# Two feed-forward layers behind banded attention on one core: another split of the tokens into chunks, and a shorter lag at the last chunk

## Chip, core and metric

The kernel runs on one NeuronCore of a Trainium2 chip. The metric is the device time of one execution in microseconds (us). PE is the matmul engine, PEld its weight loads, DVE the vector engine, ACT the scalar engine, POOL is GpSimd, and SP issues the DMAs.

## What is computed

Attention over a band of 128 keys with a linear bias (4 batches, 8 heads, 576 tokens, head size 64), then two feed-forward layers over all 2304 tokens (model width 512; hidden widths 1536 and 2048):

```python
scores = scale * np.matmul(q, k.transpose(0, 1, 3, 2))
mask = (rel >= 0) & (rel < window)                  # window = 128
scores = np.where(mask, scores + bias[None], -1000000000.0)
attn = softmax(scores)                              # over the keys
x = np.matmul(attn, v)                              # as (2304, 512)
g = x @ w_gate                                      # first layer
x = (g * sigmoid(g) * (x @ w_val)) @ w_out
h = x @ w_in                                        # second layer
y = (h * np.tanh(softplus(h))) @ w_out2
```

## The kernel before

**Layout.** The 2304 tokens lie in one row, 576 to a batch. `A_CHUNKS` (L26) cuts this row into five chunks, which attention and the first layer work off one after the other. Within a chunk, `chunk_plan` cuts queries into blocks of at most 128 that never cross a batch border; a query block sees its own 128 keys and the block ahead of it. The second layer works on three parts of 768 tokens (`TB = 384`) and is not touched.

**Attention of a chunk** (`attention`), for each of eight heads: scores (`score`; PE tile `s_ps`), a predicated copy on DVE that folds the two key blocks into one (L219 for a pair of blocks, L226 for one), a reduction on DVE (L233) and the exponential on ACT (L237) for each block, normalising (`norm`; DVE L245 and L248, then ACT L252, and in chunk 0 POOL L254 for every block but the first two), transposes on PE (`t_ps`, L259), a copy out by ACT (L265), two triangular selects on POOL (L268, L272), and for each pair of heads the product with the values (`o_ps`), from which ACT and DVE write the chunk's `xt` as a high and a low part. `S_FULL` says for how many head pairs the scores run on unsplit operands: all four of chunk 0, two of chunk 1. Elsewhere ACT and DVE first split q and k in two parts (`Q`, `K1`, `KL`).

**First layer of a chunk**: twelve hidden blocks. For each, a gate group and a value group of twelve matmuls (`gv_groups`; PE tile `g_ps`; evacuated by ACT L611 and DVE L612, then DVE L620, then split into `hh` and `hl`) and one output group of twelve matmuls (`out_group`; tile `acc`). All matmuls of these groups have as many columns as the chunk has tokens. So a chunk has 36 groups, 432 matmuls, and the five chunks together 2160.

**Order.** PE runs in the order in which the code issues (`manual_schedule`); the other engines' order is made by a scheduler. Attention of chunk 0 stands alone at the start; I call that stretch the startup. Attention of chunk c+1 is dealt out between the groups of chunk c, by cost. The weights come as 64-bit words and are converted on ACT and DVE: the pieces `convert` and `halves`, for twelve tiles `w` and six tiles `ring`, each with five large DVE instructions (L428, L421, L433, L439, L124). Three of the eighteen are asked for in the startup, the rest during the chunk-0 groups; the scheduler places some earlier than asked. From chunk 1 on the second layer's weights are converted in the gaps.

**Output groups lie back** behind their hidden block by one, and at the last chunk by `lastlag` (L34); what is then left over (`carry`) runs after the last gate group. It is PE's work while the second layer's first operands are prepared: `x_parts` writes the tiles `xs` (on ACT and DVE) for the seven products of a block in the order 1, 6, 7, 5, 2, 4, 3, and `make_win` the tiles `win` (on POOL, ACT and DVE). These tiles lie where the first layer's weights lay, so they cannot be written before its last gate groups. Products take PSUM banks in turn, every second one an `acc` bank, which the copies `ev` (L589, L590) must have emptied. `hh` and `hl` of the last chunk have `lastlag + 2` buffers each, as wide as the chunk.

Of the kernel before, what the change touches and what calls it, by code (L numbers as in the profile page):

```python
# [22 lines left out]
NF1, NF2 = F1 // 128, F2 // 128  # L23
W = 128
CT = DM // 128
A_CHUNKS = [512, 384, 512, 512, 384]  # L26
S_FULL = [4, 2, 0, 0, 0]
TB = 384
NPB = NT // (2 * TB)
# [1 line left out]

SLOT = {1: 0, 2: 1, 3: 2, 5: 3, 6: 4, 7: 5, 4: 6}
CFG = dict(
    order="SSOT", delay0=2, early=["q0", "w0", "q1", "v0", "q2", "w1", "v1", "q3", "v2", "w2", "v3"], pbufs=10, pump_g=2, pump_p=2, lag=4, lastlag=6, evprio=500,  # L34
    conv_a=0.0, conv_b=0.9,
)

# [55 lines left out]
def body(ctx: ExitStack, tc: tile.TileContext, qT, kT, vP, w1, w1o, w2, cst, yT):  # L93
# [33 lines left out]
    t = 0  # L127
    for n in A_CHUNKS:
        plansA.append(chunk_plan(t, n))
# [472 lines left out]
    def gv_groups(ci, i):  # L602
# [14 lines left out]
        def v():  # L617
# [5 lines left out]
            if ci == len(plansA) - 1:  # L623
                hh = bpool["p"].tile([128, A_CHUNKS[-1]], F32R, tag="hhb", name="hh", bufs=CFG["lastlag"] + 2)
                hl = bpool["p"].tile([128, A_CHUNKS[-1]], F32R, tag="hlb", name="hl", bufs=CFG["lastlag"] + 2)
            else:
# [446 lines left out]
```

## Time and profile before

| | |
|---|---|
| time, median of 3 runs | 968.68 us (965.79 to 971.12) |
| the profiled execution | 969.21 us, of which 967.5 us are the span |
| PE busy | 932.9 us, 96% of the span |
| DVE, ACT, POOL busy | 698.2, 525.5, 203.3 us |
| startup: 6.30 to 64.27 us, PE busy | 47.7 of 57.97 us |
| groups of chunk 0: 64.27 to 186.27 us | PE busy all of 122.00 us, DVE 104.29 us |
| groups of chunk 1: 186.27 to 284.06 us | PE busy 95.98 of 97.79 us |
| first product of the second layer | starts at 602.41 us |

The busy time of an engine in a stretch is the time in which one of its instructions was running. Matmuls overlap, so a matmul's own duration is longer than the distance from one to the next; prices of matmuls are taken from stretches with nothing else in them.

### The profile page before, as it was taken

Reading aid. Unit: us, or ns where it says so; the run is one execution under the profiler, and the core shown is the slowest. Engines: PE = TensorE matmul, PEld = TensorE weight load, DVE = VectorE, ACT = ScalarE, POOL = GpSimd, SP = SyncE. Lnnn points to the kernel's source line nnn. Section 1 sums busy time; section 2 is a strip of 40 time slices with the busy share of each in tenths; the row PEclk is TensorE's granted clock in tenths of the full one; section 3 lists DMA queues with packets and bytes.
Section 4 is the critical chain, followed back from the end, with each engine's and each line's share of the span. In section 5 each row is a group of like instructions: output and inputs, shape, how many; then the busy total and the mean of one; then the engine's idle time right before and its main releaser. Section 6 shows DMA issues by size and latency. Waiting matters only on the chain. (4 is left out here: it accounts for less than half of the span.)

```text
span 967.5 us, 14586 instructions
## 1 busy us (share of the span) xinstructions
PE 932.9 (96%) x5040; PEld 832.7 (86%) x5040; DVE 698.2 (72%) x1325; ACT 525.5 (54%) x1135; POOL 203.3 (21%) x348
## 2 busy tenths in 40 slices
PE   6879999999999999999998998899999999999998
PEld 5547788898988888887877998899999999999998
DVE  6798997688668755478533768778886788767673
ACT  6757567666666665355433445455544645454442
POOL 2440122111110221001013343552012320122000
PEclk9979999999999999999999999999999999999999
DMA  8864235376545743176404994624784247830275
GB/s 302 287 245 174 75 104 180 114 235 216 175 132 184 238 153 114 32 228 232 139 1 151 386 350 135 232 85 148 252 294 155 66 170 253 310 117 23 93 260 191
DMA packets 76921, 174.86 MB, mean 181 GB/s; under 512 B 9136, under 2 KB 52528, under 8 KB 67120
## 3 DMA queue, kind: packets, MB, share of 16 engines
q1 hardware_dynamic: 76848, 173.94, 53.8%
q8 instruction: 40, 0.66, 0.3%
q14 instruction: 33, 0.27, 0.1%
HBM read 138.25 MB, written 35.65 MB: 180 GB/s over the span
## 5 line engine op out<-in xcount | busy, mean ns | idle before, releaser
L114 PE MATMUL g_ps<-xt,w 128*128 128x512 f32 (+1 forms) x1440 | 317.2, 373 | 0.4 <-DVE t L612 0.4
L114 PEld LDWEIGHTS g_ps<-xt,w 128*128 128x128 f32 x1440 | 258.9, 189 | 37.3 <-issue 2.0
L114 PE MATMUL bk<-xs,win 128*128 128x384 f32 x1008 | 179.1, 336 | 7.2 <-DVE G L677 5.3
L114 PEld LDWEIGHTS bk<-xs,win 128*128 128x128 f32 x1008 | 174.3, 188 | 11.5 <-DVE G L677 8.7
L114 PE MATMUL bk<-op,wout 128*128 128x384 f32 x1008 | 175.6, 334 | 0.5 <-DMA wout<-w2o 0.5
L114 PEld LDWEIGHTS bk<-op,wout 128*128 128x128 f32 x1008 | 174.8, 188 | 0.9 <-issue 0.8
L114 PE MATMUL acc<-hh,ring 128*128 128x512 f32 (+1 forms) x480 | 149.1, 373 | 1.6 <-DVE ring L124 1.6
L121 ACT ACTIVATE op<-G 128x768 fp32r<-128x768 f32 x84 | 70.7, 846 | 65.7 <-PE bk L114 63.1
L114 PEld LDWEIGHTS acc<-hh,ring 128*128 128x128 f32 x480 | 89.0, 188 | 15.1 <-DVE ring L124 2.3
L124 DVE TENSOR_TENSOR op<-G,op 128x768 fp32r<-128x768 f32 x84 | 80.0, 959 | 27.0 <-ACT op L121 26.4
L268 POOL TENSOR_SCALAR_AFFINE_SELECT PT<-PT 128x256 f32<-128x256 f32 (+4 forms) x80 | 43.6, 559 | 229.5 <-ACT PT L265 229.3
L773 POOL TENSOR_TENSOR t<-w 128x256 f32<-128x256 f32 x48 | 43.1, 917 | 224.3 <-DVE win L124 207.5
L114 PE MATMUL acc<-hl,ring 128*128 128x512 f32 (+1 forms) x240 | 88.5, 369 | 1.1 <-DVE hl L124 1.1
L237 ACT ACTIVATE Pt<-Pt,sm 128x128 f32<-128x128 f32 (+1 forms) x160 | 62.6, 394 | 20.9 <-DVE sm L233 20.6
L611 ACT ACTIVATE t<-g_ps 128x512 f32<-128x512 f32 (+1 forms) x60 | 32.9, 548 | 56.9 <-PE g_ps L114 56.8
L612 DVE SCALAR_TENSOR_TENSOR t<-t,g_ps 128x512 f32<-128x512 f32 (+1 forms) x60 | 37.6, 627 | 35.6 <-ACT t L611 35.4
L677 DVE TENSOR_TENSOR G<-u,bk 128x384 f32<-128x384 f32 x72 | 38.9, 552 | 31.3 <-PE bk L114 29.2
L1017 ACT ACTIVATE G<-G 128x384 f32<-128x384 f32 x72 | 36.8, 519 | 43.2 <-DVE G L677 43.2
L620 DVE SCALAR_TENSOR_TENSOR t<-t,g_ps 128x512 f32<-128x512 f32 (+1 forms) x60 | 37.9, 631 | 27.5 <-PE g_ps L114 26.0
L121 ACT ACTIVATE hh<-t 128x512 fp32r<-128x512 f32 (+1 forms) x60 | 35.0, 583 | 38.7 <-DVE t L620 38.5
L252 ACT ACTIVATE Pt<-Pt,sm 128x128 f32<-128x128 f32 (+1 forms) x144 | 46.2, 390 | 12.8 <-DVE sm L248 12.7
L124 DVE TENSOR_TENSOR hl<-t,hh 128x512 fp32r<-128x512 f32 (+1 forms) x60 | 40.5, 675 | 14.5 <-ACT hh L121 14.0
(78 smaller groups left out, 1259.7 us busy)
## 6 DMA issues: line engine op xcount, KB each, us to landing
wout<-w2o SPq DMA_DIRECT2D x42, 1024.0 KB, 6.6
wraw<-w SPq DMA_DIRECT2D x16, 1024.0 KB, 6.3
w2o<-chl SPq DMA_DIRECT2D x16, 896.0 KB, 9.1
wst<-w SPq DMA_DIRECT2D x12, 1024.0 KB, 6.8
cw<-w1od SPq DMA_DIRECT2D x24, 512.0 KB, 3.9
w<-w2d SPq DMA_DIRECT2D x24, 512.0 KB, 3.3
w2d<-cw SPq DMA_DIRECT2D x16, 512.0 KB, 4.4
wraw<-w1o SPq DMA_DIRECT2D x6, 1024.0 KB, 5.9
```

The costliest lines, as they stand in the source:

```text
L114: nc.tensor.matmul(out=out, lhsT=lhsT, rhs=rhs, start=start, stop=stop, skip_group_check=True)
L121: return nc.scalar.activation(out=out, in_=in_, func=AF.Copy)
L124: return nc.vector.tensor_tensor(out=out, in0=in_, in1=hi.bitcast(F32), op=ALU.subtract)
L237: nc.scalar.activation(out=Pt[:q.qn], in_=Pt[:q.qn], func=AF.Exp, scale=-1.0, bias=sm[:q.qn, i:i + 1], accum_out=sm[:q.qn, 8 + i:9 + i],)
L252: nc.scalar.activation(out=pt, in_=pt, func=AF.Copy, scale=r)
L268: nc.gpsimd.affine_select(out=here, in_=prev, pattern=[[0, m], [1, n]], compare_op=ALU.is_ge, fill=0.0, base=0, channel_multiplier=-1,)
L611: tanhs.append(nc.scalar.activation(out=t[:, :n], in_=st["g"][:, :n], func=AF.Tanh, scale=0.5))
L612: nc.vector.scalar_tensor_tensor(out=t[:, :n], in0=t[:, :n], scalar=1.0, in1=st["g"][:, :n], op0=ALU.add, op1=ALU.mult)
L620: nc.vector.scalar_tensor_tensor(out=t[:, :n], in0=t[:, :n], scalar=0.5, in1=vps[:, :n], op0=ALU.mult, op1=ALU.mult)
L677: nc.vector.tensor_tensor(out=out, in0=a, in1=b, op=op)
L773: nc.gpsimd.tensor_tensor(out=x[:, o], in0=a, in1=b, op=ALU.subtract)
L1017: nc.scalar.activation(out=out, in_=in_, func=AF.Mish)
```

## The change

Two numbers change. The chunks are 384, 448, 512, 512 and 448 tokens in place of 512, 384, 512, 512 and 384, and `lastlag` is 4 in place of 6:

```diff
-A_CHUNKS = [512, 384, 512, 512, 384]
+A_CHUNKS = [384, 448, 512, 512, 448]
-    ... pump_g=2, pump_p=2, lag=4, lastlag=6, evprio=500,
+    ... pump_g=2, pump_p=2, lag=4, lastlag=4, evprio=500,
```

Query blocks in the chunks were 4, 4, 4, 5, 3 and are 3, 4, 5, 4, 4. Since the chunk borders move, so do the places at which attention, conversions and groups meet, and the scheduler deals DVE, ACT and POOL anew. Three places on DVE:

DVE at the end of the startup, before: the last instructions up to the low part of the fourth `xt`, the tile that the first gate group needs (`cw`, `cp` and `w` are a weight tile under conversion).

```order
L428 TENSOR_SCALAR cw<-wst 128x1024 x2
L433 SCALAR_TENSOR_TENSOR cw<-wst,cw 128x1024
L124 TENSOR_TENSOR xt<-o_ps,xt 128x512
L433 SCALAR_TENSOR_TENSOR cw<-wst,cw 128x1024
L439 SCALAR_TENSOR_TENSOR cw<-cw,cp 128x1024
L421 TENSOR_SCALAR cp<-cg 128x512
L439 SCALAR_TENSOR_TENSOR cw<-cw,cp 128x1024
L124 TENSOR_TENSOR w<-cw,w 128x1024
L421 TENSOR_SCALAR cp<-cg 128x512
L428 TENSOR_SCALAR cw<-wraw 128x1024
L124 TENSOR_TENSOR w<-cw,w 128x1024
L124 TENSOR_TENSOR xt<-o_ps,xt 128x512
```

The same place now, up to the fourth `xt`:

```order
L248 RECIPROCAL sm<-sm 128x3
L124 TENSOR_TENSOR w<-cw,w 128x1024
L124 TENSOR_TENSOR xt<-o_ps,xt 128x384
L428 TENSOR_SCALAR cw<-wst 128x1024
L433 SCALAR_TENSOR_TENSOR cw<-wst,cw 128x1024
L428 TENSOR_SCALAR cw<-wst 128x1024
L439 SCALAR_TENSOR_TENSOR cw<-cw,cp 128x1024
L433 SCALAR_TENSOR_TENSOR cw<-wst,cw 128x1024
L421 TENSOR_SCALAR cp<-cg 128x512
L124 TENSOR_TENSOR w<-cw,w 128x1024
L439 SCALAR_TENSOR_TENSOR cw<-cw,cp 128x1024
L124 TENSOR_TENSOR xt<-o_ps,xt 128x384
```

Five `w` and two `ring` tiles are finished ahead of the fourth `xt` or right behind it in both orders; what moved is the last reciprocal, which now stands nearer to the fourth `xt`, and the width of `xt`.

DVE late in the chunk-0 groups, before: from the tenth gate block's L612 to the eleventh's (`KL`, `Q`, `s_ps`, `sm` belong to attention, `xt` to chunk 1).

```order
L612 SCALAR_TENSOR_TENSOR t<-t,g_ps 128x512
L433 SCALAR_TENSOR_TENSOR cw<-wraw,cw 128x1024
L124 TENSOR_TENSOR xt<-o_ps,xt 128x384
L620 SCALAR_TENSOR_TENSOR t<-t,g_ps 128x512
L439 SCALAR_TENSOR_TENSOR cw<-cw,cp 128x1024
L124 TENSOR_TENSOR hl<-t,hh 128x512
L219 COPY_PREDICATED s_ps<-cst_sb,s_ps 128x2x128
L612 SCALAR_TENSOR_TENSOR t<-t,g_ps 128x512
```

The same stretch now:

```order
L612 SCALAR_TENSOR_TENSOR t<-t,g_ps 128x384
L124 TENSOR_TENSOR w<-cw,w 128x1024
L124 TENSOR_TENSOR xt<-o_ps,xt 128x448
L620 SCALAR_TENSOR_TENSOR t<-t,g_ps 128x384
L245 TENSOR_SCALAR sm<-sm 128x4
L428 TENSOR_SCALAR cw<-wraw 128x1024
L248 RECIPROCAL sm<-sm 128x4
L433 SCALAR_TENSOR_TENSOR cw<-wraw,cw 128x1024
L124 TENSOR_TENSOR hl<-t,hh 128x384
L439 SCALAR_TENSOR_TENSOR cw<-cw,cp 128x1024
L219 COPY_PREDICATED s_ps<-cst_sb,s_ps 128x2x128
L612 SCALAR_TENSOR_TENSOR t<-t,g_ps 128x384
```

The last `w` tile, which stood ahead of the tenth gate block, has moved behind it. From the seventh gate block to the thirteenth there were four L439 (one per converted tile) and are five.

DVE at the start of the second layer, before: from the third part of the first `xs` tiles to the first product's `u` (`xs_6079` is the tile of product 6, the second that PE asks for; `ev` empties the bank that it writes).

```order
L124 TENSOR_TENSOR xs_6075<-xr,xs_6075 128x768
L677 TENSOR_TENSOR xr<-xr 128x2x384
L124 TENSOR_TENSOR win<-t_6074,win 128x1024
L124 TENSOR_TENSOR xs_6079<-xr,xs_6079 128x768
L124 TENSOR_TENSOR win<-w_6111,win 128x768
L590 COPY ev<-acc_5765 128x384
L124 TENSOR_TENSOR xs_6081<-xr,xs_6081 128x768
L590 COPY ev<-acc_5767 128x384
L124 TENSOR_TENSOR win<-t_6074,win 128x1024
L677 TENSOR_TENSOR u<-u,bk 128x384 x2
```

The same stretch now (product 6's tile is `xs_6132`):

```order
L124 TENSOR_TENSOR win<-t_6127,win 128x1024
L677 TENSOR_TENSOR xr<-xr 128x2x384
L124 TENSOR_TENSOR xs_6128<-xr,xs_6128 128x768
L590 COPY ev<-acc_5699 128x448
L124 TENSOR_TENSOR win<-w_6164,win 128x768
L590 COPY ev<-acc_5701 128x448
L677 TENSOR_TENSOR xr<-xr 128x2x384
L124 TENSOR_TENSOR xs_6132<-xr,xs_6132 128x768
L124 TENSOR_TENSOR win<-t_6127,win 128x1024
L124 TENSOR_TENSOR xs_6134<-xr,xs_6134 128x768
L677 TENSOR_TENSOR u<-u,bk 128x384 x2
```

Product 6's tile, which stood ahead of both `ev`, now stands behind them. Between the last gate group and the first product PE had 84 matmuls of 384 columns (seven output groups) and has 60 of 448 (five).

## Rows read from the trace of the kernel before

**Rows 1.** The page: busy tenths of PE in 40 equal slices of the span

```profile
PE   6879999999999999999998998899999999999998
```

**Rows 2.** Windows: length; busy (instructions) of PE, PEld, DVE, ACT, POOL; clock; DMA; GB/s

```profile
6.30:64.27 57.97, 47.70 (x161) 31.21 (x161) 48.43 (x135) 42.67 (x112) 27.14 (x40) 0.89 0.85 304
...
45.76:66.30 20.54, 13.57 (x55) 7.57 (x54) 20.27 (x35) 14.81 (x31) 12.16 (x14) 0.67 0.69 251
...
64.27:186.27 122.00, 122.00 (x614) 94.40 (x613) 104.29 (x244) 79.13 (x210) 21.61 (x58) 1.00 0.42 135
...
186.27:284.06 97.79, 95.98 (x613) 90.84 (x612) 73.38 (x186) 62.84 (x166) 14.40 (x24) 1.00 0.61 187
```

**Rows 3.** Windows of two groups of twelve with nothing between: 384 and 512 columns

```profile
253.47:257.74 4.27, 4.27 (x25) 4.27 (x25) 3.51 (x11) 3.04 (x11) 0.00 (x0) 1.00 0.41 141
...
305.40:311.01 5.61, 5.61 (x29) 4.62 (x26) 5.20 (x14) 3.38 (x9) 0.00 (x0) 1.00 0.85 285
```

**Rows 4.** Timeline of PE, startup: start, us, line, tiles, count, idle before

```profile
32.29 3.35 PE L114 MATMUL s_ps<-qkv 64*128 64x256 f32 x8
...
35.57 1.11 PE L259 MATMUL t_ps<-cst_sb,Pt 128*128 128x128 f32 x4
...
39.90 3.25 PE L114 MATMUL o_ps<-PT,qkv 128*64 128x256 f32 x16
...
64.27 3.30 PE L114 MATMUL g_ps<-xt,w 128*128 128x512 f32 x12
```

**Rows 5.** Timeline of DVE, startup

```profile
8.38 0.43 DVE L219 COPY_PREDICATED s_ps<-cst_sb,s_ps 128x256 f32<-128x256 uint8 x1 [8.38 <-PE s_ps L114]
...
45.76 0.42 DVE L219 COPY_PREDICATED s_ps<-cst_sb,s_ps 128x256 f32<-128x256 uint8 x1
...
52.54 0.18 DVE L248 RECIPROCAL sm<-sm 128x4 f32<-128x4 f32 x1
...
65.70 0.68 DVE L124 TENSOR_TENSOR xt<-o_ps,xt 128x512 fp32r<-128x512 f32 x1
```

**Rows 6.** Timeline of POOL, startup

```profile
33.84 0.64 POOL L272 TENSOR_SCALAR_AFFINE_SELECT PT<-PT 128x512 f32<-128x512 f32 x1
...
52.21 2.89 POOL L254 TENSOR_SCALAR Pt<-Pt,sm 128x128 f32<-128x128 f32 x4 [2.47 <-DVE sm L248]
...
57.85 3.18 POOL L272 TENSOR_SCALAR_AFFINE_SELECT PT<-PT 128x512 f32<-128x512 f32 x2
```

**Rows 7.** Groups by form: busy us, mean ns, idle before and its releaser

```profile
L233 DVE CUSTOM_DVE_ANT_0 Pt<-s_ps,cst_sb 128x128 f32<-128x128 f32 x128 | 33.0, 283 | 4.8 <-PE t_ps L259 3.6
...
L226 DVE COPY_PREDICATED s_ps<-cst_sb,s_ps 128x128 f32<-128x128 uint8 x32 | 9.3, 290 | 5.8 <-PE s_ps L114 5.6
...
L612 DVE SCALAR_TENSOR_TENSOR t<-t,g_ps 128x512 f32<-128x512 f32 x36 | 24.5, 680 | 23.9 <-ACT t L611 23.7
...
L612 DVE SCALAR_TENSOR_TENSOR t<-t,g_ps 128x384 f32<-128x384 f32 x24 | 13.1, 546 | 11.7 <-ACT t L611 11.7
```

**Rows 8.** Windows of the tile s_ps, then t_ps: groups of chunks 1 and 3

```profile
186.27:284.06 97.79, 10.43 (x68) 9.71 (x68) 14.32 (x52) 1.00 0.61 187
...
404.09:522.38 118.29, 6.40 (x36) 5.78 (x36) 8.84 (x30) 0.99 0.37 124
...
186.27:284.06 97.79, 4.79 (x32) 3.98 (x32) 4.71 (x8) 1.00 0.61 187
...
404.09:522.38 118.29, 3.91 (x24) 3.11 (x24) 3.82 (x8) 0.99 0.37 124
```

**Rows 9.** Timeline of PE, last pair of heads of the last chunk

```profile
511.02 1.49 PE L114 MATMUL o_ps<-PT,v 128*64 128x256 f32 x13 [2.47 <-POOL PT L272]
```

**Rows 10.** Timeline, start of the second layer

```profile
586.46 2.69 DVE L124 TENSOR_TENSOR xs<-xr,xs 128x768 fp32r<-128x768 f32 x3
...
600.95 1.21 DVE L124 TENSOR_TENSOR win<-t,win 128x1024 fp32r<-128x1024 f32 x1
...
604.51 3.36 PE L114 MATMUL bk<-xs,win 128*128 128x384 f32 x18 [0.89 <-DVE ev L590]
```

More of the change, by code (lines that the diff above doesn't have):

```diff
@@ L33 @@
 CFG = dict(
-    order="SSOT", delay0=2, early=["q0", "w0", "q1", "v0", "q2", "w1", "v1", "q3", "v2", "w2", "v3"], pbufs=10, pump_g=2, pump_p=2, lag=4, lastlag=6, evprio=500,
+    order="SSOT", delay0=2, early=["q0", "w0", "q1", "v0", "q2", "w1", "v1", "q3", "v2", "w2", "v3"], pbufs=10, pump_g=2, pump_p=2, lag=4, lastlag=4, evprio=500,
     conv_a=0.0, conv_b=0.9,
```

## The prediction

> **What bounds the kernel now.** I read the page's slices first: PE is busy almost throughout except in the first three slices [rows 1]. So away from the start the sum of PE's work sets the time, and edits on other engines count only where they stop PE. The windows show two kinds of stretch [rows 2]. In the startup PE is busy for 47.7 of 57.97 us, and in its last 20.54 us DVE is busy for 20.27: there DVE, not PE, sets the pace. In the groups of chunk 0 PE is busy all 122.00 us, but DVE 104.29, so DVE has only 15% to spare. In the groups of chunk 1 it has a quarter to spare, and PE still loses 1.8 us.
>
> **The change part by part.** The sum is made against the profiled execution, 969.2 us, 0.5 above the median.
>
> *Matmuls of the first layer.* Two groups of twelve take 4.27 us at 384 columns and 5.61 at 512 [rows 3], 0.0111 and 0.0110 us a column. On this line 448 columns take 4.94. A chunk has 18 such pairs; before 18 x (3 x 5.61 + 2 x 4.27), now 18 x (4.27 + 2 x 4.94 + 2 x 5.61): the same. No row shows 448 columns. If it cost what 512 does, 36 pairs x 0.67 = 24 us would come on top, if what 384 does, 24 would go; I take the line, since both rows lie on it through zero. Term: 0.
>
> *Startup.* Chunk 0 has three query blocks instead of four; per head 640 score columns instead of 896. Scores of a head take 3.35 us, transposes 1.11, the product of a pair 3.25 [rows 4]; at 640/896 and 3/4 they become 2.39, 0.83 and 2.32. To the end of the eighth head's scores PE has 8 scores, 5 transposes and 2 products: 38.9 us, now 27.9. DVE reaches the eighth head's copy at 45.76 [rows 5], with 48.43 - 18.2 = 30.2 us of work behind it [rows 2]. It loses 7 x (0.29 + 0.28) = 4.0 [rows 7], but in the new order one xt and most of a further converted tile stand ahead of that copy, some 2.8, so DVE still needs 29. From 8.38 on that is 37.4; PE's own sum from 6.30, with the 3 us that it waited, gives 37.5. Both are near, so I put the copy at 39: 6.8 earlier. From there to the first gate group are 18.5 us [rows 4, 5]: 6.8 to the last reciprocal, then POOL's scaling, transposes, POOL's selects and the last product. Now the reciprocal comes after about 5.4; behind it POOL scales one block per head instead of two (four took 2.89, so -1.5), the selects are a quarter narrower (two took 3.18, two more stand ahead of them, so -1.1) [rows 6], the product is 0.9 shorter: -4.9 in all. That walk gives -11.7. The bounds: if DVE alone sets the pace, it has 8 x 0.57 + 4 x 0.13 = 5.1 less to do [rows 7], so -5.1; if everything shrinks with the blocks, a quarter of 57.97, so -14.5. I take -10.3, a little off the walk, because DVE was busy for 98.7% of the stretch's end.
>
> *Groups of chunk 0.* PE's 35 groups in this window shrink by 0.67 each [rows 3], 23.5 us, and attention of chunk 1 grows by 1.3 (448 tokens for 384, a twelfth more score columns): 122.0 becomes 99.8. DVE's 104.3 falls only by 24 x 0.13 [rows 7] and gains about 1: 102. The weight conversions stay, and there the cover ends. With the 98.7% at which DVE ran under pressure [rows 2] the stretch needs 103.4, +3.6 over PE's own sum; and the order puts a fifth L439 behind the seventh gate block, where there were four, so the pressure falls late. Who waits is PE: for PSUM banks that L612 and L620 empty, and for scores that L219 has folded. I take +4. Bounds: 0, if what is late is worked off in the groups of chunk 1, where DVE has 24 us to spare; +9, if the moved tile's five instructions (about 5 us) come on top.
>
> *Where a page speaks against this.* POOL's select takes 0.64 us at 33.84, but 1.59 on average at 57.85, where DVE has no pause [rows 2, 6]. The Trainium skill, "SBUF — State Buffer", section "SBUF: two separate sides", says that VectorE and GpSimd share one port pair, which an instruction holds to its end while the other engine is shut out. The trace agrees that selects stretch beside a full DVE, by 0.95 each. What that does in a fuller stretch is the second rival.
>
> *Attention behind later groups.* Chunk 2's grows from four blocks to five and chunk 3's shrinks from five to four: these cancel. Chunk 4's grows from three to four. The same step shows between the groups of chunk 3 (three blocks) and of chunk 1 (four): scores 6.40 to 10.43, transposes 3.91 to 4.79 [rows 8], +4.9. PE is the bound there, so nothing covers it. With the 1.3 above already in the 99.8 I count 1.3 + 4.9 = 6.2 at most, 4 at least (busy times of short matmuls overlap with their neighbours): +5.
>
> *Waits that shrink.* In chunk 1's groups PE has 97.79 + 12 + 2 us for a DVE that hardly grows; of the 1.8 us lost one goes: -1 (0 to -1.8). At the last pair of heads PE waited 2.47 us for POOL [rows 9], because the last head's transposes stood directly ahead of the product; now an output group (2.8) stands between, but selects of two heads: -1 (0 to -2.5).
>
> *Lag 4.* Between the last gate group and the second layer PE has five output groups of 448 columns, 12.3 us, where it had seven of 384, 14.9. (The two others run earlier; the sum is the same.) DVE's chain in that time starts with the first xs at 586.46 and lets the second product start at 604.51, 18 us later [rows 10]. In the new order the tile of product 6, that PE's second product needs, stands behind both ev, one ring conversion (1.2) less ahead and one more win; so the second product starts about as late as before, with 2.6 us less of PE's work done: +2. Bounds: 0, if the tiles come 2.6 earlier; +5, if POOL and DVE stretch each other.
>
> **Sum:** 0 - 10.3 + 4 + 5 - 1 - 1 + 2 = -1.3, so 967.9 for an execution like the profiled one and, 0.5 lower, 967.4 for the median. I say 967.5. A measurement of this kernel can tell about 0.5% (4.8 us) from no change, so 963.8 to 973.5 counts as the same.
>
> **Rivals.** *The startup shrinks with its blocks and DVE catches up.* -14.5 in the startup, 0 in chunk 0's groups: -1.3 - 4.2 - 4 = -9.5, 959 by the median. For it: 10 us of the startup are PE's idle time, and DVE too had waits ahead of 45.76. Against it: DVE's 98.7% at the end. *DVE chokes chunk 0's groups, and POOL behind it.* Each odd head's six selects stand between its transposes and the pair's product. In chunk 0's groups PE's cover there falls from two groups and a score at 512 columns (6.1) to the same at 384 (4.7). If three of six selects stretch by the 0.95 of [rows 6], 2.9 us, and about 0.5 is left of the cover, each of four pairs waits 2.4 us: +9.6, 977. It decides as soon as DVE's work passes PE's, 102 against 99.8, on which side it lies; against it: 24 us spare in the next groups, and no product in chunk 0's groups waited before (PE busy 122.00 of 122.00). It is the lock of the page named above, priced by rows. *Only DVE's sum shrinks in the startup:* -5.1 in place of -10.3: 972.6, still the same. *448 columns cost like 512:* +24, 991; then the change doesn't leave the matmuls alone as its column count says.
>
> **How the numbers follow.** My forecast 0.40; startup in full 0.26; DVE's sum alone 0.16; the choked groups 0.16; 448 like 512 0.02. The first and third lie within 0.5%: 0.56 the same; 0.26 faster; 0.18 slower. The forecast's own range, from the bounds of its terms taken half way, is 963 to 972. To hold the time 8 times in 10 the range reaches into both neighbours and leaves out their outer halves: 958 to 976.
>
> **What would show each step.** Right: the first gate group starts near 54 us (59 means DVE's sum alone, 50 the full shrink); chunk 1's first gate group follows 104 us later, with some 4 us of PE idle before it (0 or 13 would be the rivals); pairs of 448-column groups take 4.94; the groups of chunk 3 last 4 to 5 us longer; the second product of the second layer starts 18 us after the last gate group's end. Wrong would be the whole reckoning if PE showed gaps in chunks 2 and 3, which I take as untouched, or if the second layer after its first block took another time than before.

## Result, and the profile after

The changed kernel takes 976.35 us (median of 4 runs, 975.67 to 978.96), the kernel before 967.57 in the runs beside it: ratio 1.008, 95% interval 1.0055 to 1.0105. It is slower by 0.8%, where I forecast 967.5 and no change. The profiled execution took 975.99 us, with a span of 973.8 (967.5 before).

A stage runs from the first gate group of a chunk to that of the next; the startup is counted from 6.30 us on. Lengths in us, from the starts of matmuls in the trace:

| stage | before | after | change | forecast |
|---|---|---|---|---|
| startup | 58.0 | 53.9 | -4.1 | -10.3 |
| groups of chunk 0 | 122.0 | 108.1 | -13.9 | -18.2 |
| both together | 180.0 | 162.0 | -18.0 | -28.5 |
| groups of chunk 1 | 97.8 | 110.6 | +12.8 | |
| groups of chunk 2 | 120.0 | 119.5 | -0.5 | |
| groups of chunk 3 | 118.3 | 118.4 | +0.1 | |
| chunk 4 to the first product | 80.0 | 90.1 | +10.0 | |
| second layer | 365.1 | 367.0 | +1.9 | +2 |
| all behind chunk 0's groups | 781.2 | 805.5 | +24.3 | +27.2 |

So what came later went slightly better than the forecast, and what was missed lies wholly ahead of chunk 1: 10.5 us. The windows of these two stages (columns as in [rows 2], which they answer):

```profile
6.30:60.16 53.86, 35.80 (x121) 23.50 (x121) 44.26 (x109) 35.72 (x94) 17.88 (x32) 0.87 0.87 316
60.16:168.30 108.14, 103.13 (x618) 93.17 (x617) 100.45 (x241) 77.47 (x212) 25.74 (x57) 0.98 0.47 152
```

DVE's work is what I had reckoned: 44.26 + 100.45 = 144.7, against 48.43 - 5.1 + 102 = 145.3. But I had it done in 151.5 us, and it took 162.0.

**The end of the startup.** The chain of waits that ended with the first gate group, in order of time (start, us, what):

```profile
43.17 0.80 ACT cg L416
43.97 7.89 DMA wraw<-w1o
...
52.90 0.48 ACT PT L265
...
53.45 2.21 POOL PT L268 x2
55.67 1.47 POOL PT L272
...
57.18 3.05 PE o_ps L114 x10
60.23 1.94 PE g_ps L114 x10
```

A DMA of 7.89 us stands in a chain where the forecast had only DVE, POOL and PE. ACT works its queue in order; the first step (`cg`, L416) of converting the third ring tile waits there for its weights, and behind it stand the copies (L265) of the last two heads' transposes. The timelines of ACT, PE and DVE show it:

```profile
51.89 1.11 ACT L416 ACTIVATE cg<-wraw 128x1024 bf16<-128x1024 bf16 x1 [2.24 <-DMA wraw<-w1o]
52.90 0.86 ACT L265 ACTIVATE PT<-t_ps 128x384 f32<-128x384 f32 x2
...
49.05 1.25 PE L259 MATMUL t_ps<-cst_sb,Pt 128*128 128x128 f32 x6
57.18 3.05 PE L114 MATMUL o_ps<-PT,qkv 128*64 128x256 f32 x12 [6.87 <-POOL PT L272]
...
41.60 0.42 DVE L219 COPY_PREDICATED s_ps<-cst_sb,s_ps 128x256 f32<-128x256 uint8 x1
47.06 0.18 DVE L248 RECIPROCAL sm<-sm 128x3 f32<-128x3 f32 x1
```

The transposes end at 50.3, their copies start at 52.90.

**The groups of chunk 0.** PE waits six times here, 5.0 us in all, 4.5 of them for DVE; before it had no wait. A stretch of the stage, then PE's longest waits, then DVE ahead of the first of them:

```profile
110.00:143.00 33.00, 27.99 (x165) 25.23 (x164) 32.21 (x79) 23.00 (x62) 11.23 (x21) 0.95 0.48 153
```

```profile
116.07 0.35 PE L114 MATMUL s_ps<-K,Q 128*128 128x256 f32 x1 [2.13 <-DVE Q L193]
136.84 0.36 PE L114 MATMUL s_ps<-K,Q 128*128 128x256 f32 x1 [1.16 <-DVE Q L193]
138.05 0.38 PE L114 MATMUL s_ps<-KL,Q 128*128 128x256 f32 x1 [0.85 <-DVE KL L124]
...
113.12 0.68 DVE L428 TENSOR_SCALAR cw<-wst 128x1024 int32<-128x1024 int32 x1
113.72 0.54 DVE L612 SCALAR_TENSOR_TENSOR t<-t,g_ps 128x384 f32<-128x384 f32 x1
114.18 0.75 DVE L124 TENSOR_TENSOR KL<-kraw,K 128x576 fp32r<-128x576 f32 x1
114.85 0.41 DVE L421 TENSOR_SCALAR cp<-cg 128x512 int32<-128x512 int32 x1
115.30 0.62 DVE L193 SCALAR_TENSOR_TENSOR Q<-qraw,Q 64x448 fp32r<-64x448 f32 x1
```

From 110 to 143 DVE is busy for 32.21 of 33 us; from 143 on PE waits no more. The split of the next head's queries (`Q`) stands in its queue behind conversion steps, and PE's scores wait for it.

### The profile page after: what moved, and what is told of

Its sections match the earlier page's. It is cut to its first block, busy times and chain, and to the rows that moved or that the text cites. A ratio compares the mean times of both kernels' runs of the same rounds, so it can differ in the third digit from the quotient of the medians.

```text
span 973.8 us, 14616 instructions
## 1 busy us (share of the span) xinstructions
PE 928.3 (95%) x5040; PEld 839.6 (86%) x5040; DVE 696.1 (71%) x1317; ACT 527.7 (54%) x1151; POOL 205.6 (21%) x356
## 3 DMA queue, kind: packets, MB, share of 16 engines
q1 hardware_dynamic: 76848, 174.33, 53.9%
## 4 chain that ended last, share of the span: by engine, by line
PE 74%; DMA 9%; DVE 9%; ACT 3%; issue 2%; POOL 2%; SPq 1%; DVEq 0%; ACTq 0%; POOLq 0%
PE bk L114 33%; PE g_ps L114 24%; PE acc L114 11%; DMA wraw<-w 5%; PE s_ps L114 3%; PE o_ps L114 2%; DMA wraw<-w1o 1%; PE t_ps L259 1%; DVE cw L433 1%; DVE G L677 1%; POOL t L773 1%; DMA x2d<-ev 1%; DMA wst<-w 1%; DVE win L124 1%; DMA w2d<-cw 1%
## 5 line engine op out<-in xcount | busy, mean ns | idle before, releaser
L114 PE MATMUL g_ps<-xt,w 128*128 128x448 f32 (+2 forms) x1440 | 316.4, 372 | 0.4 <-DVE t L620 0.3
L114 PEld LDWEIGHTS g_ps<-xt,w 128*128 128x128 f32 x1440 | 261.7, 188 | 34.0 <-issue 1.9
L114 PEld LDWEIGHTS bk<-xs,win 128*128 128x128 f32 x1008 | 175.8, 189 | 12.8 <-DVE G L677 9.7
L114 PE MATMUL acc<-hh,ring 128*128 128x448 f32 (+2 forms) x480 | 150.9, 377 | 0.0
L268 POOL TENSOR_SCALAR_AFFINE_SELECT PT<-PT 128x384 f32<-128x384 f32 (+4 forms) x88 | 47.0, 554 | 253.4 <-ACT PT L265 253.4
L124 DVE TENSOR_TENSOR op<-G,op 128x768 fp32r<-128x768 f32 x84 | 79.8, 957 | 27.1 <-ACT op L121 26.6
L114 PE MATMUL acc<-hl,ring 128*128 128x448 f32 (+2 forms) x240 | 89.6, 373 | 0.0
L237 ACT ACTIVATE Pt<-Pt,sm 128x128 f32<-128x128 f32 (+1 forms) x160 | 62.7, 394 | 24.9 <-DVE sm L233 23.5
L612 DVE SCALAR_TENSOR_TENSOR t<-t,g_ps 128x448 f32<-128x448 f32 (+2 forms) x60 | 37.8, 629 | 45.6 <-ACT t L611 45.5
L611 ACT ACTIVATE t<-g_ps 128x448 f32<-128x448 f32 (+2 forms) x60 | 32.9, 548 | 50.4 <-PE g_ps L114 50.4
L620 DVE SCALAR_TENSOR_TENSOR t<-t,g_ps 128x448 f32<-128x448 f32 (+2 forms) x60 | 37.9, 631 | 29.9 <-PE g_ps L114 28.9
L121 ACT ACTIVATE hh<-t 128x448 fp32r<-128x448 f32 (+2 forms) x60 | 35.0, 584 | 44.1 <-DVE t L620 44.1
L252 ACT ACTIVATE Pt<-Pt,sm 128x128 f32<-128x128 f32 (+1 forms) x152 | 48.8, 393 | 10.4 <-DVE sm L248 10.3
L114 PEld LDWEIGHTS acc<-hl,ring 128*128 128x128 f32 x240 | 45.6, 190 | 5.0
```

The lines of the kernel that those rows point to most:

```text
L114: nc.tensor.matmul(out=out, lhsT=lhsT, rhs=rhs, start=start, stop=stop, skip_group_check=True)
L121: return nc.scalar.activation(out=out, in_=in_, func=AF.Copy)
L124: return nc.vector.tensor_tensor(out=out, in0=in_, in1=hi.bitcast(F32), op=ALU.subtract)
L237: nc.scalar.activation(out=Pt[:q.qn], in_=Pt[:q.qn], func=AF.Exp, scale=-1.0, bias=sm[:q.qn, i:i + 1], accum_out=sm[:q.qn, 8 + i:9 + i],)
L252: nc.scalar.activation(out=pt, in_=pt, func=AF.Copy, scale=r)
L268: nc.gpsimd.affine_select(out=here, in_=prev, pattern=[[0, m], [1, n]], compare_op=ALU.is_ge, fill=0.0, base=0, channel_multiplier=-1,)
```

## Experiments

All ratios are against the kernel before on the same chip. The stages are those of the profiled execution, the median that of all; "both" is startup plus groups of chunk 0.

| kernel | startup | groups of chunk 0 | both | median, ratio (95%) |
|---|---|---|---|---|
| before | 58.0 | 122.0 | 180.0 | |
| after | 53.9 | 108.1 | 162.0 | 976.35, 1.008 (1.0055 to 1.0105) |
| e1 old chunks, lag 4 | 59.5 | 122.1 | 181.6 | 970.37, 1.0011 (0.9988 to 1.0034) |
| e2 384 first | 48.0 | 115.3 | 163.4 | 976.28, 1.0078 (1.0043 to 1.0113) |
| e3 448 last | 57.9 | 122.3 | 180.2 | 967.53, 0.9992 (0.9973 to 1.0010) |
| e4 new, ACT reordered | 48.7 | 112.4 | 161.1 | 975.98, 1.0083 (1.0054 to 1.0111) |
| e5 new, less DVE | 48.9 | 105.1 | 154.0 | 970.21, 1.0029 (0.9993 to 1.0065) |
| e6 old, less DVE | 52.2 | 123.5 | 175.7 | 968.65, 0.9996 (0.9983 to 1.0010) |
| e7 old, hold | 53.2 | 125.6 | 178.8 | 966.19, 0.9971 (0.9949 to 0.9994) |
| e8 new, hold | 47.8 | 120.5 | 168.3 | 979.32, 1.0111 (1.0090 to 1.0132) |
| e9 448 first | 62.3 | 117.6 | 179.8 | 985.61, 1.0166 (1.0133 to 1.0200) |
| e10 hold, 448 last | 50.3 | 124.9 | 175.2 | 963.68, 0.9938 (0.9915 to 0.9961) |
| e11 old, weak hold | 51.6 | 128.5 | 180.1 | 967.37, 0.9984 (0.9962 to 1.0006) |
| e12 new, least DVE | 41.1 | 113.2 | 154.2 | 968.19, 1.0005 (0.9975 to 1.0034) |
| e13 old, least DVE | 55.7 | 122.6 | 178.2 | 974.78, 1.0056 (1.0037 to 1.0075) |

### Which part of the change costs (e1 to e3)

```diff
-lastlag=6
+lastlag=4
```

> The old chunks (512, 384, 512, 512, 384) with the new lag of 4 at the last chunk: the second edit alone. My theory: the second product of the second layer starts about 18 us after the last gate group's end whatever PE has to do until then; with five output groups of 384 columns (10.7 us) in place of seven (14.9), PE loses what is missing: 3 to 4 us more idle time behind the first product, 971 to 972 us. Rival (the tiles for the second product come earlier because fewer output groups stand ahead of them): no change, 967 to 968. Nothing ahead of the last chunk should move in either.

```diff
-A_CHUNKS = [512, 384, 512, 512, 384]
+A_CHUNKS = [384, 512, 512, 512, 384]
```

> Chunks 384, 512, 512, 512, 384 with lag 6: the first chunk alone is shortened, its 128 tokens go to the second; the last chunk and the lag stay as before. My theory (the loss lies at the front: a startup that shrinks by 4 us only, and chunk-0 groups in which DVE is full): first gate group near 60; the chunk-0 groups last 110 us or more, with PE idle for 6 to 10 us behind DVE's splits and evacuations, since the second chunk has five query blocks instead of four and DVE some 6 us more to do; in all 975 to 977 us. Rival (the loss comes with the longer last chunk and its shorter lag): the front gives its gain, 964 to 968 us.

```diff
-A_CHUNKS = [512, 384, 512, 512, 384]
+A_CHUNKS = [512, 384, 512, 448, 448]
-lastlag=6
+lastlag=4
```

> Chunks 512, 384, 512, 448, 448 with lag 4: the last chunk alone is lengthened, by tokens of the fourth, and the lag is 4; the first three chunks stay. My theory (front loss): startup and chunk-0 groups last as before (58 and 122 us); the last pair of heads no longer stops PE (2.5 us less), the entry into the second layer costs some 2 us more: 966 to 970 us. Rival (the loss lies in the last chunk): 974 to 977 us.

The short first chunk, with its 128 tokens moved to the second, loses as much as the whole change (976.28); the long last chunk with lag 4 loses nothing (967.53). The rival is out. In e2 I had expected the first gate group near 60; it starts at 54.34, and e4 below shows why. In e1 PE waits twice ahead of the second product's work:

```profile
603.60 0.41 PE L114 MATMUL bk<-xs,win 128*128 128x384 f32 x1 [1.76 <-DVE ev L590]
607.92 22.22 PE L114 MATMUL bk<-xs,win 128*128 128x384 f32 x113 [3.91 <-DVE xs L124]
```

With 1.35 at a ring tile that is 7.0 us, against 0.94 + 0.70 + 0.89 + 1.05 = 3.6 before: the lag alone costs the 3.4 us at this place that were expected. Chunk 1's groups were 2 us shorter in that execution, and the whole time leaves it at 1.0011, not to be told from no change: 970.37 lies between the two expectations.

### The ACT queue (e4)

```diff
-                nc.scalar.activation(
+                mark["pt", ci, h] = nc.scalar.activation(
...
+        if r == 2:
+            cg = fs[0]
+
+            def held():
+                with tc.issue_after(mark["pt", 0, H - 1].ins):
+                    cg()
+
+            fs[0] = held
```

> The changed kernel (384, 448, 512, 512, 448, lag 4) in which the first conversion step of the third ring tile, an ACT instruction that waited 2.24 us for its weights ahead of the copies of the last two heads' transposes, is queued on ACT behind these copies; its order there changes, no work. My theory for the startup (ACT's queue holds back the last heads): the copies start near 50.4 instead of 52.9 and the first gate group near 58 instead of 60.2. For the whole, theory A (what the startup gains stays): 974 us, 2 less than the changed kernel. Theory B (the chunk-0 groups are DVE's, so the gain is given back there): 976 us, with the chunk-0 groups longer by what the startup is shorter.

ACT, POOL, then DVE at the end of the startup, and PE in its first gate group:

```profile
48.93 1.07 ACT L265 ACTIVATE PT<-t_ps 128x384 f32<-128x384 f32 x2 [0.40 <-PE t_ps L259]
51.74 1.13 ACT L417 ACTIVATE cg<-wraw 128x1024 bf16<-128x1024 bf16 x1 [1.75 <-DMA wraw<-w1o]
...
50.17 1.39 POOL L272 TENSOR_SCALAR_AFFINE_SELECT PT<-PT 128x384 f32<-128x384 f32 x1
51.51 0.52 POOL L268 TENSOR_SCALAR_AFFINE_SELECT PT<-PT 128x384 f32<-128x384 f32 x1
...
49.75 1.42 DVE L434 SCALAR_TENSOR_TENSOR cw<-wst,cw 128x1024 f32<-128x1024 uint32 x1
53.00 0.69 DVE L429 TENSOR_SCALAR cw<-wst 128x1024 int32<-128x1024 int32 x1 [1.83 <-DMA w1od<-cw]
...
59.09 0.62 PE L114 MATMUL g_ps<-xt,w 128*128 128x384 f32 x2 [2.11 <-DVE xt L124]
```

(e4 adds a line further up, so L417 here is L416 elsewhere, and L434 is L433.)

The copies no longer wait for the DMA, and the startup falls to 48.7 us: 5.2 less (1.1 of it was gained ahead of the transposes), and 1.0 from the forecast's 47.7. (In e2 the scheduler happened to put the step behind the copies too: 48.0.) Yet the whole gains nothing. The groups of chunk 0 take 112.4, and chunk 1 starts at 167.4 instead of 168.3: theory B. Of the 5.2 us, 2.1 are lost again in the first gate group itself: its last two matmuls wait for the fourth `xt`, which stands behind conversion steps on DVE. So the late startup was a real error of the forecast, but not what makes the kernel slower.

### DVE's work (e5, e6, e12, e13)

These kernels leave out a part of the conversion, so only their times count.

```diff
-    ... scalar1=0xFFFFF, scalar2=0x100000, ...
+    ... scalar1=0, scalar2=1, ...
...
-    out=st["w"], in0=st["w"], scalar=2.0 ** -20, in1=st["p"],
+    out=st["w"][:, :8], in0=st["w"][:, :8], scalar=2.0 ** -20, in1=st["p"][:, :8],
```

> The changed kernel with less work on DVE: in each weight conversion the last multiply (L439, 1.21 us) is done on 8 columns instead of 1024, about 1.1 us less in each of the 18 first-layer tiles (and of the 32 second-layer ones later); the scale of the weights is left out with it, and the mask ahead of it is made a constant, so that the numbers stay finite. Theory A (DVE's queue is what stops PE until chunk 1): startup and chunk-0 groups together, 162.0 us in the changed kernel, fall by 8 us or more, to 154 or less, PE's waits for Q, KL and t vanish and chunk-0 groups come near PE's own 100 to 102 us. Theory B (the waits come from the order of attention's steps, not from the sum on DVE): 160 or more.

> The same shortened multiply (the same part of the computation left out) in the kernel before. Theory A: its chunk-0 groups were PE's (122.0 us) and stay; only the startup gains, 1 to 5 us; so the old split gains less than the new one, and the new one is then level with or ahead of the old. Theory B: both gain the same.

In e12 and e13 L433 is cut in the same way:

```diff
-    out=st["w"], in0=words[:, :, 0].bitcast(U32), ... in1=st["w"].bitcast(I32),
+    out=st["w"][:, :8], in0=words[:, :8, 0].bitcast(U32), ... in1=st["w"][:, :8].bitcast(I32),
```

> The changed kernel with still less work on DVE: the third and the last step of each weight conversion (L433 and L439, 1.2 us each) are done on 8 columns instead of 1024, some 2.2 us less in each tile; the weights' low words and scale are left out with it. Theory A (my sum for startup and chunk-0 groups, 151.5 us, failed only because DVE could not keep up): startup 46 to 50, chunk-0 groups 100 to 102.5, together 147 to 152. Theory B (DVE's sum is not all; order or POOL stops PE as well): 153 or more together.

> The same in the kernel before (the same part of the computation left out). Theory A: the chunk-0 groups stay PE's, 122 us, the startup 50 to 53, together 172 to 175; the new split is then ahead by the 3 to 5 us that the forecast's sum had without the groups' +4: the changed kernel at 0.995 to 1.0 of this one. Theory B: both gain the same against their own kernels and the new split stays behind by 5 us or more.

e5 is best read against e4, since their startups agree (48.9 and 48.7): the groups of chunk 0 fall from 112.4 to 105.1. Here is that window of e5:

```profile
55.22:160.31 105.09, 101.15 (x617) 91.62 (x617) 90.57 (x244) 77.78 (x212) 20.71 (x57) 1.00 0.54 175
```

To leave the startup's accidents aside, count from the first output product to chunk 1 (the order here: before, after, e4, e8, e5, e12):

```profile
79.24:186.27 107.03, 107.03 (x554) 83.97 (x553) 90.66 (x216) 71.17 (x194) 21.61 (x58) 1.00 0.41 129
...
72.09:168.30 96.21, 91.20 (x558) 83.16 (x557) 89.18 (x217) 70.02 (x197) 25.74 (x57) 0.98 0.45 144
...
69.30:167.37 98.07, 91.65 (x558) 84.06 (x558) 88.43 (x216) 71.07 (x199) 23.73 (x57) 0.97 0.46 143
...
66.96:174.56 107.60, 97.46 (x558) 87.62 (x557) 99.74 (x232) 76.44 (x202) 32.62 (x57) 0.92 0.53 173
...
69.11:160.31 91.20, 88.71 (x557) 81.43 (x557) 76.91 (x214) 69.26 (x196) 20.71 (x57) 1.00 0.48 146
...
68.84:160.50 91.66, 89.70 (x557) 82.81 (x557) 69.18 (x211) 68.60 (x197) 18.83 (x57) 0.98 0.46 141
```

With 77 or 69 us of DVE work this stretch takes 91 to 92 us, with 89 us 96 to 98, with 99.7 us 107.6. In all three loaded cases DVE is busy for 90 to 93% and PE waits. (In e8 the granted clock is 0.92 in this stretch, so PE's own work is longer there too, 97.46 us.) So it is mostly DVE's sum that stops PE in the new split (theory A); in the old one PE is busy for all 107 us with 90.66 us of DVE work beside it, and less of it (e6, e13) leaves the groups at 123.5 and 122.6.

The sum is not all, though. e5's groups were to come near 100 to 102 us, with no waits for `Q` and `KL`: they take 105.1, and 0.77 and 0.81 us of these waits are left. And the longest wait of the changed kernel, 2.13 us for `Q`, is still there in e12, where DVE is busy for only 75% of the stretch:

```profile
112.58 0.38 PE L114 MATMUL s_ps<-K,Q 128*128 128x256 f32 x1 [1.91 <-DVE Q L193]
```

That wait comes more from DVE's order than from its sum: `Q` stands there behind a step of 1.22 us (L124, a `w` tile).

By the medians, new against old goes from +8.8 us to +1.6 with a step left out, which is not to be told from level, and to -6.6 with two (of the profiled executions: +6.3, +1.1, -1.7; e12's was the slowest of its ten). So the new split stands the better against the old, the less DVE has to do. That it would then beat the kernel before is not shown: e12 takes 968.19 for 968.75. Both lost time in the groups of chunks 2 and 3, e12 10.7 us against after and e13 11.5 against before. There DVE, with less to do, stands before conversion steps whose weights have not come: 3.8 us in all before and 6.3 after, but 17.7 in e12 and 23.1 in e13. One of them in e13, on DVE, and the wait of PE behind it (`Q` stands in DVE's queue after that step):

```profile
323.51 0.70 DVE L428 TENSOR_SCALAR cw<-wraw 128x1024 int32<-128x1024 int32 x1 [6.38 <-DMA wraw<-w]
...
328.28 0.39 PE L114 MATMUL s_ps<-K,Q 128*128 128x256 f32 x1 [3.29 <-DVE Q L193]
```

e12 takes 154.2 for both, not 147 to 152, which is theory B's number. Its startup is short (41.1), but then the same kind of ACT wait comes at the first gate groups, and behind it a stretch at the lower clock (ACT, PE, and a window with the granted clock in the column ahead of DMA's share):

```profile
50.14 1.11 ACT L416 ACTIVATE cg<-wraw 128x1024 bf16<-128x1024 bf16 x1 [4.92 <-DMA wraw<-w1o]
...
52.70 1.60 PE L114 MATMUL g_ps<-xt,w 128*128 128x384 f32 x3 [3.18 <-ACT xt L121]
...
56.00:66.00 10.00, 10.00 (x32) 8.56 (x32) 5.06 (x19) 3.43 (x11) 0.00 (x0) 0.54 0.99 376
```

In e13 the startup gained 2.3 us instead of 5 to 8; PE waits there 6.28 us for POOL's selects ahead of the last product. e6's gained 5.8 where I had said 1 to 5, yet its whole time is level with before: its groups of chunk 3 take 5.4 us longer. So I read these runs by the stage first and by the whole time second.

### Holding conversions back (e7, e8, e11, e10)

```diff
-        return [f1, f2, f3, f4, f5]
+        def behind(f, k):
+            def g():
+                with tc.issue_after(mark[k, 0, H - 1].ins):
+                    f()
+
+            return g if (k, 0, H - 1) in mark else f
+
+        return [behind(f1, "pt"), behind(f2, "rc"), behind(f3, "rc"), f4, f5]
```

> The kernel before, with all weight conversions but the first three kept out of the startup: their first steps are queued on ACT behind the last head's copies and on DVE behind the last head's reciprocal. DVE has then some 18 us less to do in the startup and 18 us more in the chunk-0 groups, where it had 17.7 us to spare. Theory A (DVE's sum up to chunk 1 counts, and in the kernel before it had 27 us of idle time in these 180): startup about 50 us, chunk-0 groups 125 to 128, in all 964 to 967 us. Theory B (what the startup gains is given back in full): 968 to 970.

> The same hold in the changed kernel. Its chunk-0 groups are 24 us shorter and have no room for 18 us more of DVE work. Theory A: startup 42 to 46 us, chunk-0 groups 116 to 120, the sum 160 to 164 as in the changed kernel (162.0): 974 to 978 us, no better than without the hold. Theory B (the startup is what costs the new split its gain): 968 or less.

The new split has no room for the work pushed out of the startup: its groups grow to 120.5, and it becomes the slowest but one, 979.32. That is worse than theory A, which had 160 to 164 for both (168.3) and 974 to 978. The old split takes it with 3.6 us more in the groups and 4.8 less in the startup (53.2, where I had said 50); its time is theory A's (966.19).

```diff
-            return g if (k, 0, H - 1) in mark else f
+            return g if (k, 0, H - 1) in mark and len(nconv) > 5 else f
```

> The kernel before with a weaker hold: the third weight tile and the second ring tile may again be converted in the startup, only the tiles after these are held behind the last head of chunk 0. Theory A (DVE's idle time in the startup can be filled without delaying the last head): startup 54 to 57, chunk-0 groups 122 to 124, sum 177 to 179, 965 to 967 us. Theory B (what matters is that nothing stands ahead of the last reciprocal): the sum is 180 as before, 968 to 969.

The sum is 180.1, theory B's number, but not by its mechanism: the startup fell by 6.4 us, more than theory A had, and the groups of chunk 0 grew by 6.5. In them the first gate groups wait 2.5 us for `xt`, and from 62 to 79 the granted clock is 0.80. The whole time (967.37) lies between the two, so e11 decides nothing.

> Chunks 512, 384, 512, 448, 448 with lag 4, and the hold of the later conversions behind the last head of chunk 0: the two variants that were not behind the kernel before, put together. If their gains add (startup and chunk-0 groups about 1 us less, the last chunks about 2 us less): 964 to 966 us. If they do not: 967 to 969.

e10 is e3's chunks and lag with e7's hold. The gains add, and a little more: 963.68 us, just under the expected 964 to 966, and 0.9938 of the kernel before, the whole interval below 1. It beats both kernels. More came at the front than expected, 4.8 us for both instead of 1; why more than in e7 was not followed.

### Half the step (e9)

```diff
-A_CHUNKS = [512, 384, 512, 512, 384]
+A_CHUNKS = [448, 448, 512, 512, 384]
```

> Chunks 448, 448, 512, 512, 384 with lag 6: half the step at the front, nothing changed at the end. PE's own sum for the chunk-0 groups is 122.0 - 18 x 0.67 + 1.3 = 111.2 us, DVE's about 104, 93% of it. Theory A (what counts up to chunk 1 is DVE's queue, which the new split stops at some 162 us): startup 55 to 58, chunk-0 groups 111 to 114, and 12 us more in the chunk-1 groups: 967 to 971 us, so most of the loss of the full step is absent. Theory B (every shorter first chunk loses in the same measure): half the loss of the full step or more, 972 us and up.

Theory A missed. The time lies in theory B's open range, 972 and up, but half the step loses nearly twice what the whole one does, so its mechanism is not shown either: this is the slowest of all. The window of its startup, and PE's waits in the last pairs of heads:

```profile
6.30:68.57 62.27, 43.40 (x160) 24.30 (x159) 46.84 (x134) 41.31 (x119) 37.01 (x56) 0.80 0.80 281
```

```profile
57.59 1.28 PE L259 MATMUL t_ps<-cst_sb,Pt 128*128 128x128 f32 x4 [4.20 <-ACT Pt L252]
60.95 1.11 PE L114 MATMUL o_ps<-PT,qkv 128*64 128x256 f32 x2 [2.08 <-POOL PT L272]
65.50 3.14 PE L114 MATMUL o_ps<-PT,qkv 128*64 128x256 f32 x14 [3.44 <-POOL PT L272]
```

POOL is busy for 37.01 us with 56 instructions; before it was 27.14 with 40 [rows 2]. 448 tokens are three blocks of 128 and one of 64; the code treats blocks of another width as a run of their own, so a head needs two copies and four selects instead of one and two. The startup grew by 4.3 us, and the gain in the groups only paid that back. The longest wait, 4.20, is for ACT's normalising. Whether POOL's extra work alone did it was not tried. e9's groups of chunk 1 are 12.5 us longer, as the changed kernel's are (12.8), with no gain ahead of them to pay for it.

## Why the prediction was wrong, step by step

**Matmuls: right.** Two gate groups of 448 columns, with nothing between, in the last chunk:

```profile
524.29:529.09 4.80, 4.80 (x25) 4.50 (x24) 3.22 (x5) 1.58 (x3) 0.92 (x2) 1.00 1.08 383
```

4.80 us; in like places a pair takes 4.16 at 384 and 5.50 at 512 columns, so 448 lies on the line, and the rival with +24 us is out. My 4.94 was a little high: in both windows of [rows 3] the first matmul took 0.11 us longer up to the next than the others. Only differences entered the sum.

**Startup: -10.3 forecast, -4.1 measured.** The walk held as far as it was about DVE: from the eighth head's copy to the last reciprocal 5.46 us, where I said 5.4. It failed at two places, both ACT's queue with a conversion step that waited for its weights. At the first, the step waited 4.03 us for the first weight tile (2.74 before) ahead of the scaling of the second pair's queries, and PE 2.93 for that; the eighth head's copy came at 41.60 instead of 39. At the second, the last heads' copies came 2.6 us late, and all four selects then ran beside a busy DVE. I had weighed DVE, POOL and PE and named no wait on ACT for a DMA. Where the second wait is away, the term was right to 1 us (48.7 in e4, 48.0 in e2, for 47.7), counted to the first matmul of the gate group; its last two then wait 2.1 us for DVE's `xt` in both. That -4.1 is close to the rival "only DVE's sum shrinks" is chance: another cause gave its number.

**Groups of chunk 0: +4 forecast, +8.3 measured (108.1 over 99.8), and +12.6 in e4,** where the startup is as forecast. This is the step that made the sign. I took the two terms as independent, -10.3 and +4, although one queue pays both: a part of what the startup leaves over on DVE arrives in the groups (in e4 DVE has 4.5 us less work than after in the startup and 2.3 more in the groups). I also took from a 20 us stretch that DVE under pressure works 98.7% of the time; over this whole stage it reached 92.9% (100.45 of 108.14); the trace has its instructions wait for PE and ACT in between. Of the 8.3 us, PE's waits are 5.0, not far from my 4; the other 3.3 are PE's own work, 103.13 for my 99.8. Some 1.5 of that is the lower clock behind two of the waits (last section); the rest I had counted too low, as e5's 101.15 at a clock of 1.00 shows. In e4 the waits are 8.5: what the startup gains, the groups wait. And I had noted that the fifth converted tile falls late, which is where it hit (110 to 143 us), but booked it as a bound.

**Rivals.** "DVE chokes chunk 0's groups, and POOL behind it" gave 977, close to the result, with a mechanism that is half right: DVE does choke them, but PE waits for `Q`, `KL` and `t`, and no product there waits for POOL's selects. That selects stretch beside a busy DVE shows in e4's rows: a select took 0.52 us at 51.51, when DVE stood idle, and one of the same shape 1.39 at 50.17, beside L434, which reads two tiles in SBUF. This agrees with the Trainium skill, "SBUF — State Buffer", section "SBUF: two separate sides" (one port pair, held by one of the two engines for a whole instruction). It lengthened the startup's end, not the groups.

**Attention behind later groups: +5 forecast.** In chunk 1 scores and transposes grew by 1.9 us, in chunk 2 they shrank by 1.9, as I said. Chunk 3's scores and transposes grew from 6.40 and 3.91 [rows 8] to 7.45 and 5.56, 2.7 us instead of 4.9: mis-sized, and below the 4 that I had named as the least. (The most, 6.2, counted the 1.3 of chunk 1 a second time.) One sign of being wrong did show, a gap of PE in chunk 2's groups, 1.79 us at 316.28 behind ACT's copy of `PT`; the stage is 0.5 us shorter even so.

**Waits that shrink.** In chunk 1 one wait of 0.83 is left of 1.8 us. At the last pair of heads I gave 1 us and more came back: before, the clock fell behind the wait of 2.47 [rows 9]. The window of the place, then of the two groups ahead of it, and the same place after:

```profile
507.90:519.64 11.74, 9.27 (x41) 6.75 (x41) 3.42 (x4) 4.72 (x7) 4.50 (x6) 0.85 0.00 0
498.90:504.40 5.50, 5.50 (x26) 4.46 (x25) 0.69 (x1) 0.60 (x1) 0.00 (x0) 1.00 0.00 0
```

```profile
499.00:516.00 17.00, 17.00 (x89) 13.64 (x88) 7.50 (x10) 7.48 (x13) 7.63 (x12) 1.00 0.02 3
```

The two groups that follow the wait took 6.77 us where two others took 5.50; after, PE has no wait there. So chunk 3 lasts as long as before (118.4), where I expected it 4 to 5 us longer.

**Lag 4: right in size, in part by luck.** PE, ACT and DVE at the entry of the second layer:

```profile
611.02 5.30 PE L114 MATMUL bk<-xs,win 128*128 128x384 f32 x29 [2.77 <-DVE xs L124]
620.42 16.15 PE L114 MATMUL bk<-xs,win 128*128 128x384 f32 x84 [4.10 <-DVE G L677]
...
617.59 1.06 ACT L121 ACTIVATE win<-t 128x1024 fp32r<-128x1024 f32 x1 [3.82 <-POOL t L773]
618.55 0.47 ACT L1017 ACTIVATE G<-bk 128x384 f32<-128x384 f32 x1
```

PE goes on at 611.02, 16.6 us after the last gate group's end (18 forecast). The second wait of 4.10 I had not seen: ACT's `win` waits for POOL's differences, the `G` that frees a bank stands behind it, and DVE and PE follow; up to 625 the granted clock is then 0.69. The second layer takes 1.9 us longer, where I said 2, but it is made up otherwise: PE goes on 1.4 us earlier than I said, and the second wait takes that back.

## What to carry to other kernels

Terms that draw on one engine can't be added stage by stage: take the engine's whole work up to the next boundary, and the share of time that it reached over a long stretch (90 to 93% here), not the 99% of a short one. An instruction that waits for a DMA on an in-order queue delays everything behind it, so when compute shrinks ahead of a fixed transfer, look for the queue in which that transfer is awaited. A shorter stage is worth what its fullest engine can give up, and not what the matmuls lose. And a wait for one tile can outlast the load: look where that tile stands in the engine's queue before calling the engine full.

## What I had not expected of the hardware

A short wait of PE can cost more than its own length, when the granted clock falls to half behind it, the lower level of 1.2 GHz. So it was behind the waits at 136.84 and 138.05, but not behind the longer one of 2.13 us that ended at 116.07 (window of the output group behind the two waits, then of the stretch behind the longer one; the clock stands ahead of DMA's share):

```profile
138.51:142.16 3.65, 3.65 (x14) 3.61 (x13) 3.62 (x11) 0.51 (x1) 1.20 (x3) 0.53 0.50 128
...
116.07:119.00 2.93, 2.93 (x20) 2.89 (x20) 2.93 (x9) 1.72 (x7) 2.35 (x4) 1.00 0.40 103
```

The output group took 3.65 us at 0.53; others of its kind here take 2.10. Two waits of 2.0 us together cost 1.5 more in this way, and the wait of 2.47 before some 1.3. In e12 the first gate groups ran at 0.54 for 10 us, after 8.65 us in which PE had been busy for 5.47. So the length of a wait alone does not tell whether the clock falls.
